# Moving the transposed keys of a gated linear attention forward, waiting for their transfers with one column product, and fixing SyncE's order

## The chip, the cores and the metric

The kernel runs on one core of a Trainium2 chip. Its engines are TensorE (matrix products; the profile shows it as PE, and its weight loads as PEld), VectorE (DVE), ScalarE (ACT), GpSimd (POOL) and SyncE (SP), each with its own queue of instructions that is worked off in order. DMAs are issued from the queues of SP, ACT and POOL. The metric is the time of one execution on the device in microseconds (us).

## The reference

Two blocks follow each other. The first is an attention with a state: for each of 4 batches and 8 heads, with 768 positions and 48 dimensions, a 48x48 state decays by a gate per row and takes up an outer product at every position. The second is a feed-forward net with a leaky activation on the 3072 rows that come out.

```python
def _attn_ref(q, k, v, f_logit):                    # (4, 8, 768, 48) each
    f = 1.0 / (1.0 + np.exp(-f_logit))
    state = np.zeros((B, H, D, D), dtype=np.float32)
    for t in range(S):
        state = f[:, :, t, :, None] * state + np.einsum('bhd,bhe->bhde', k[:, :, t], v[:, :, t])
        y[:, :, t] = np.einsum('bhd,bhde->bhe', q[:, :, t], state)

def _moe_ref(x, w_in, w_out, alpha):                # (3072, 384), (384, 2048), (2048, 384)
    h = x @ w_in
    g = np.maximum(h, 0.0) + alpha * np.minimum(h, 0.0)
    return g @ w_out
```

## The kernel before

**Steps and stages.** The work is cut into 12 steps. A step is a pair of batches (`bp`, 0 or 1) and a chunk of 128 positions (`c`, 0 to 5); the steps run over the chunks, and within a chunk over the two pairs, so that a pair's state is needed again two steps later. Each step has four stages, written as Python generators that yield between pieces:

- `prepare` (letter P; Q is the same for the next step) loads f, q, k and v, takes the sigmoid on ScalarE, and has VectorE make the decayed queries and keys. Its pieces: loads and lagged queries (lines 264 to 296), two scans (317, 319), the products q4 and k4 (321, 347), the decayed keys `ended(0)` into `kh` and `ended(1)` into half of `ks`, among the products `us` (L330) and `q3` (L368); then the other half of `ks` (L398), and, for chunks after the first, a transpose of the 32x32 blocks of `ks` into `kt` (L401); then copies into A on ScalarE (L419) and the transfers of `kt` into `ksn` (L427).
- `carry` (O): products of the half chunks (`off`, L444), then in a second piece the products that update the state (`pd`, L484), 32 small matmuls (each two records in the profile) that read `ksn` and v; VectorE adds them to the state in `vs` (`moved`, L494 and L498).
- `attend` (S): products within blocks (`raw` L520, `qu` L535), their masked copies on VectorE (L526, L541) and ScalarE (L563), the output `py` (L574), its copy `y` (L583), and ten transfers that turn y into rows `xT` for the net (L603), shared out over the queues of SP, ACT and POOL.
- `network` (n) of the step before: eight groups `ph0` to `ph7` of six matmuls with w_in (L618), the activation on ScalarE (L623) and VectorE (L625), then seven products with w_out by a scheme that saves one of eight (`pa` to `pe`, L657), sums (L661, L678), and two stores (L633).

**The transfers of the keys.** `kt` holds the keys with 32x32 blocks transposed; 16 small DMAs on SP put the blocks where the products pd want them. `ksn` has one buffer, and `y` is allocated under the same tag: the transfers of one step wait until the y of the step before has been read by its ten xT transfers, and that y waits for the pd before it.

**Order.** `FIRST` and `USUAL` (lines 31 to 37) spell the order of the pieces: four first steps by themselves, then the usual one. In the step of `USUAL` a step's attention stands between the pieces of the net of the step before and of the preparation of the next. Inside `tc.manual_schedule` (L734) TensorE, VectorE and ScalarE run in just this order; SP and POOL are ordered by a scheduler. The DMAs of loads are issued by POOL, but for the first step's, which SP issues (L262).

**Waits.** A matmul holds one semaphore wait itself; further ones stand in front of it as wait instructions (EVENT_SEMAPHORE) in TensorE's queue, each with up to two. DMAs count on 8 semaphores in turn, so that a DMA also waits for the one eight before it.

**PSUM.** The tag `net` has four banks (ph, pa to pe), the tag `pair` two double banks (raw, qu, off, pd, py).

Of the kernel before, what the change touches and what calls it, by code (L numbers as in the profile page):

```python
# [8 lines left out]
F32 = mybir.dt.float32  # L9
# [18 lines left out]
RAWS, LEADS = 5, 4  # L28
UP = 2.0 ** 16

FIRST = (
# [4 lines left out]
)  # L36
USUAL = "S n2 S n2 O2 n Q n3 Q n Q S3 n Q S n Q n Q n"

def flat(first, usual, steps=12):
    out = []  # L40
    left = {}
    for n in range(steps + 1):
        for key in (first[n] if n < len(first) else usual).split():
            for _ in range(int(key[1:] or 1)):
                k = key[0]
                if k in "awbvW":
                    out.append((k,))
                else:
                    m = n - 1 if k == "n" else n + 1 if k == "Q" else n
                    k = "P" if k == "Q" else k  # L50
                    if 0 <= m < steps:
                        out.append((k, m))
    return out
# [5 lines left out]
def kernel(  # L59
# [65 lines left out]
    def bank(name):  # L125
        return psn.tile([128, 512], F32, tag="net", name=name)
# [131 lines left out]
    def prepare(bp, c, x):  # L258

        i = f"{bp}_{c}"  # L260
        b0 = U * bp
        loads = nc.gpsimd if bp or c else nc.sync  # L262

        def load(name, src, bufs=2):
            t = work.tile([128, W], F32, tag=name, name=f"{name}_{i}", bufs=bufs)
# [105 lines left out]
        def ended(j):  # L371
            js = slice(j, G, 2)
            kj = ks[:, :, 1] if j else kh
            nc.vector.tensor_tensor(kj.rearrange("p g (i r) -> p g i r", r=4),
                                    k4.rearrange("p (g i r) -> p g i r", i=NB, r=4)[:, js],
                                    suf[:, js].unsqueeze(3).broadcast_to((128, GC, NB, 4)), ALU.mult)

        ended(0)
        if c:
            earlier(3)  # L380
        else:
            near(2, 1)
        ended(1)
        if c:
            earlier(4)
        else:
# [8 lines left out]
        yield  # L395
        if c:
            earlier(6)
        nc.vector.tensor_tensor(ks[:, :, 0], kh, f32[:, 1:G:2].broadcast_to((128, GC, DB)), ALU.mult)  # L398
        if c:
            kt = x["kt"] = late["kt"].tile([128, W], F32, tag="kt", name=f"kt_{i}")  # L400
            nc.vector.transpose(kt, ks.rearrange("p g s t -> p (g s t)"))  # L401
            earlier(7)
        else:
            nc.vector.tensor_tensor(q16.rearrange("p g (i r) -> p g i r", r=4), q4[:, :, NQ:NB], g16[:, :, NQ:NB].unsqueeze(3).broadcast_to((128, G, NQ, 4)), ALU.mult)
# [12 lines left out]
        for cc in range(0 if c else 1, NC2):  # L417
            for par in range(2):
                nc.scalar.copy(A[halves(cc)[1], :, par * HP:(par + 1) * HP, CH * cc:CH * (cc + 1)],  # L419
                               q3[rows(par)].rearrange("p (u h c) s t -> p u h c (s t)", h=HP, c=NC2)[:, :, :, cc, 0:CH])  # L420
        if c:
            kt = x["kt"]
            ksn = x["ksn"] = work.tile([128, U, HP * 128], F32, tag="ksn", name=f"ksn_{i}", bufs=1)
            for a in range(4):
                n = min(32, D - 32 * (a % 2))
                for b in range(NJ):
                    nc.sync.dma_start(  # L427
                        out=ksn[32 * b:32 * (b + 1)].rearrange("p u (h x) -> p (u h) x", h=HP)[:, :, 32 * a:32 * a + n],
                        in_=kt[32 * a:32 * (a + 1)].rearrange("p (g b x) -> p g b x", b=NJ, x=32)[:, :, b, 0:n])
        yield  # L430

    def carry(bp, c, x):
# [176 lines left out]
    def network(bp, c, x):  # L609
        i = f"{bp}_{c}"  # L610
        xT = x["T"]
        plain = (bp, c) == steps[0]
        for f in range(NH):
            ph = bank(f"ph{f}_{i}")
            tiles = (2 * f, 2 * f + 1) if plain else (f, f + NH)
            for kt in range(NK):
                for j, m in enumerate(tiles):
                    nc.tensor.matmul(ph[:, j * T:(j + 1) * T], lhsT=w_in_sb[:, kt, m * 128:(m + 1) * 128],  # L618
                                     rhs=xT[:, kt], start=(kt == 0 and j == 0), stop=(kt == NK - 1 and j == 1),
                                     skip_group_check=True)  # L620
            neg = work.tile([128, 2, T], F32, tag="neg", name=f"neg{f}_{i}")
            phv = ph.rearrange("p (j t) -> p j t", j=2)
            nc.scalar.activation(neg, phv, AF.Relu, scale=-1.0)  # L623
            for j, m in enumerate(tiles):
                nc.vector.scalar_tensor_tensor(gate[:, m % NH, m // NH], neg[:, j], om[:, m:m + 1], phv[:, j],  # L625
                                               ALU.mult, ALU.add)
            if not plain and f % 4 == 3:
                sums(slice(f - 3, f + 1))
            yield

        def store(u, o):
            t0 = ((U * bp + u) * NC + c) * C
            nc.sync.dma_start(out=out[t0:t0 + C], in_=o)  # L633

        if plain:
            po = [bank(f"po{u}_{i}") for u in range(U)]
            for n, (f, u) in enumerate([(f, u) for f in range(NF) for u in range(U)]):
                nc.tensor.matmul(po[u][:, 0:DM], lhsT=gate[:, f % NH, f // NH, u * C:(u + 1) * C], rhs=w_out_sb[:, f],  # L638
                                 start=(f == 0), stop=(f == NF - 1))
                if n % 8 == 7 and n != U * NF - 1:  # L640
                    yield
            for u in range(U):
                o = work.tile([128, DM], F32, tag="o", name=f"o{u}_{i}")
                nc.scalar.activation(o, po[u][:, 0:DM], AF.Copy, scale=UP)
                store(u, o)
            yield
            return

        a11, a12, a22 = (lambda f, j=j, u=u: gate[:, f, j, u * C:(u + 1) * C] for j, u in ((0, 0), (1, 0), (1, 1)))
        s1, s2, s3, s4 = (lambda f, n=n: late["S"][:, n, f] for n in range(4))  # L650
        b11, t1, b21, b22 = (lambda f, r=r, d=d: w_out_sb[:, NH * r + f, DH * d:DH * (d + 1)]
                             for r, d in ((0, 0), (0, 1), (1, 0), (1, 1)))
        t2, t3, t4 = (lambda f, t=t: late[t][:, f] for t in ("t2", "t3", "t4"))

        def product(to, of, by, more=False):
            for f in range(NH):
                nc.tensor.matmul(to[:, 0:DH], lhsT=of(f), rhs=by(f), start=(f == 0 and not more), stop=(f == NH - 1),  # L657
                                 skip_group_check=True)

        def plus(to, of, by, scale=UP):  # L660
            nc.vector.scalar_tensor_tensor(to, of[:, 0:DH], scale, by, ALU.mult, ALU.add)  # L661

        o0, o1 = (work.tile([128, DM], F32, tag="o", name=f"o{u}_{i}") for u in range(U))
        kept, u2, u3 = (late["C"][:, n] for n in range(3))
        pa, pb = (bank(f"p{n}_{i}") for n in "ab")
        product(pa, a11, b11)
        product(pb, a22, t4)
        nc.scalar.activation(kept, pa[:, 0:DH], AF.Copy, scale=UP)
        yield
        pc, pd = (bank(f"p{n}_{i}") for n in "cd")  # L670
        product(pc, s2, t2)
        product(pd, s1, t1)
        plus(u2, pc, kept)
        yield
        product(pa, a12, b21, more=True)
        product(pc, s3, t3, more=True)
        plus(o0[:, DH:DM], pd, u2)
        nc.scalar.activation(o0[:, 0:DH], pa[:, 0:DH], AF.Copy, scale=UP)  # L678
        yield
        pe = bank(f"pe_{i}")  # L680
        product(pe, s4, b22)
        plus(u3, pc, kept)
        plus(o1[:, 0:DH], pb, u3, -UP)
        plus(o1[:, DH:DM], pd, u3)
        store(1, o1)
        yield
        plus(o0[:, DH:DM], pe, o0[:, DH:DM])
        store(0, o0)
        yield

    late = {}

    def sums(fs_):

# [36 lines left out]

    pieces["W"] = halves_of_w_out()

    with tc.manual_schedule(engines={mybir.EngineType.PE, mybir.EngineType.DVE, mybir.EngineType.Activation}):  # L734
        for _ in range(IDLE):
            nc.tensor.matmul(idle[0:32, 0:8], lhsT=ones[:, 0:32], rhs=ones[:, 0:8], start=True, stop=True)
        run = {}
        for n, step in enumerate(steps):
            x = {}
            for key, stage_ in zip("POSn", (prepare, carry, attend, network)):  # L740
                run[key, n] = stage_(*step, x)
        for key in order:
            next(run[key] if key in run else pieces[key[0]])
# [55 lines left out]
```

## Time and profile before

| | |
|---|---|
| median of 3 runs | 621.78 us (621.24 to 621.89) |
| span of the profiled execution | 622.1 us |
| instructions in the profile | 19062 |
| ScalarE's share of the chain that ended last | 3% |
| HBM read, written | 36.21 MB, 4.72 MB |

The profile is one execution. It gives busy time per engine, a timeline of instructions, the chain of work that ended last, and for each group of instructions (by line, engine and tile) what ended the idle time before it. A row such as `pd<-vs,ksn` means that the tile pd is written from vs and ksn. A matmul of 32-bit numbers shows as two records. A "q" behind an engine's name (PEldq, SPq) marks work of its sequencer: waits and the issue of DMAs.

Where the loads and transfers stand in the profile before, by its list of DMA issues (KB each, median us from issue to landing):

| transfer | issued by | count | KB | us |
|---|---|---|---|---|
| f | POOL | 11 | 512 | 4.5 |
| q | POOL | 11 | 512 | 4.2 |
| k | POOL | 11 | 512 | 4.9 |
| v | POOL | 22 | 192 | 4.6 |
| ksn from kt | SP | 80 | 32 | 2.0 |
| out | SP | 24 | 192 | 2.7 |

The list groups by shape; the ksn transfers of the other shape, as many again, are not among its eight lines.

### The profile page before, as it was taken

Reading aid. Unit: us, or ns where it says so; the run is one execution under the profiler, and the core shown is the slowest. Engines: PE = TensorE matmul, PEld = TensorE weight load, DVE = VectorE, ACT = ScalarE, POOL = GpSimd, SP = SyncE. Lnnn points to the kernel's source line nnn. Section 1 sums busy time; section 2 is a strip of 40 time slices with the busy share of each in tenths; the row PEclk is TensorE's granted clock in tenths of the full one; section 3 lists DMA queues with packets and bytes.
Section 4 is the critical chain, followed back from the end, with each engine's and each line's share of the span. In section 5 each row is a group of like instructions: output and inputs, shape, how many; then the busy total and the mean of one; then the engine's idle time right before and its main releaser. Section 6 shows DMA issues by size and latency. Waiting matters only on the chain.

```text
span 622.1 us, 19062 instructions
## 1 busy us (share of the span) xinstructions
PE 592.1 (95%) x8212; PEld 529.8 (85%) x8212; DVE 497.1 (80%) x997; ACT 246.6 (40%) x466; POOL 63.0 (10%) x117
## 2 busy tenths in 40 slices
PE   3568999999999999999999999999999999999997
PEld 3457866898899899899899899899889889889997
DVE  7588998899898798798798798798888888762261
ACT  5677862441641272262261351352253243223110
POOL 9120010001000011001001001001001000000000
PEclk9999999999999999999999999999999999999999
DMA  9964632014404314214313313413313401201000
GB/s 290 367 234 155 190 85 52 36 36 108 98 8 96 72 35 107 67 35 95 79 35 90 84 35 88 86 36 86 87 36 85 87 3 26 53 2 27 26 0 26
DMA packets 68116, 50.43 MB, mean 81 GB/s; under 512 B 47168, under 2 KB 60608, under 8 KB 68032
## 3 DMA queue, kind: packets, MB, share of 16 engines
q1 hardware_dynamic: 56656, 25.01, 15.6%
q0 software_dynamic: 6864, 22.35, 12.7%
q10 hardware_dynamic: 4512, 1.85, 1.7%
q8 instruction: 65, 1.06, 0.7%
q14 instruction: 19, 0.16, 0.1%
HBM read 36.21 MB, written 4.72 MB: 66 GB/s over the span
## 4 chain that ended last, share of the span: by engine, by line
PE 88%; DVE 6%; ACT 3%; issue 2%; DMA 1%; ACTq 0%; DVEq 0%
PE ph L618 39%; PE pc L657 9%; PE pa L657 8%; PE pd L657 5%; PE pe L657 4%; PE pb L657 4%; PE py L574 4%; PE po L638 3%; PE raw L520 3%; PE qu L535 3%; PE pd L484 3%; PE off L444 1%; PE xt L592 1%; DVE gate L625 1%; DMA f<-in_fT 1%
## 5 line engine op out<-in xcount | busy, mean ns | idle before, releaser
L618 PE MATMUL ph<-xT,w_in_sb 128*128 128x256 f32 x1152 | 258.7, 382 | 0.7 <-DVE Csum L661 0.7
L618 PEld LDWEIGHTS ph<-xT,w_in_sb 128*128 128x128 f32 x1152 | 216.4, 190 | 33.4 <-issue 2.3
L623 ACT ACTIVATE neg<-ph 128x512 f32<-128x512 f32 x96 | 57.4, 598 | 200.8 <-PE ph L618 139.5
L625 DVE SCALAR_TENSOR_TENSOR gate<-neg,om,ph 128x256 f32<-128x256 f32 x192 | 82.7, 478 | 50.6 <-ACT neg L623 50.4
L657 PE MATMUL pc<-t,S 128*128 128x192 f32 x352 | 61.7, 329 | 0.0
L657 PE MATMUL pa<-w_out_sb,gate 128*128 128x192 f32 x352 | 61.3, 327 | 0.1
L657 PEld LDWEIGHTS pa<-w_out_sb,gate 128*128 128x128 f32 x352 | 57.9, 190 | 1.0 <-DVE gate L625 0.4
L657 PEld LDWEIGHTS pc<-t,S 128*128 128x128 f32 x352 | 57.3, 190 | 0.6
L526 DVE COPY_PREDICATED ad<-mraw,raw 128x256 f32<-128x256 int32 (+1 forms) x96 | 42.4, 442 | 11.1 <-PE raw L520 8.6
L541 DVE COPY_PREDICATED ad<-mquad,qu 128x224 f32<-128x224 int32 (+6 forms) x140 | 42.0, 300 | 6.2
L419 ACT COPY A<-q 48x512 f32<-48x512 f32 x44 | 27.2, 619 | 36.1 <-DVE q L368 35.7
L563 ACT COPY A<-ad 32x256 f32<-32x256 f32 x96 | 38.7, 403 | 1.4
L330 DVE TENSOR_TENSOR us<-us,fs 128x768 f32<-128x768 f32 (+5 forms) x60 | 36.8, 614 | 0.0
L678 ACT ACTIVATE o<-pa 128x192 f32<-128x192 f32 x11 | 3.7, 332 | 75.2 <-PE pa L657 72.3
L661 DVE SCALAR_TENSOR_TENSOR Csum<-pc,Csum 128x192 f32<-128x192 f32 x22 | 7.9, 357 | 30.3 <-PE pc L657 30.1
L287 DVE TENSOR_TENSOR qd<-qd,f 128x768 f32<-128x768 f32 (+2 forms) x36 | 27.2, 756 | 6.0 <-ACT qd L282 6.0
L520 PEld LDWEIGHTS raw<-qd,k 48*32 48x32 f32 x1536 | 18.5, 109 | 15.3 <-issue 13.1
L520 PE MATMUL raw<-qd,k 48*32 48x80 f32 x1536 | 24.0, 243 | 7.6 <-issue 4.4
L702 DVE TENSOR_TENSOR S<-gate 128x512 f32<-128x512 f32 x44 | 30.3, 688 | 0.8
L657 PE MATMUL pe<-w_out_sb,S 128*128 128x192 f32 x176 | 30.4, 326 | 0.0
L657 PE MATMUL pd<-w_out_sb,S 128*128 128x192 f32 x176 | 30.4, 326 | 0.0
L657 PE MATMUL pb<-t,gate 128*128 128x192 f32 x176 | 30.4, 326 | 0.0
(101 smaller groups left out, 758.3 us busy)
## 6 DMA issues: line engine op xcount, KB each, us to landing
w_out_raw<-in_w_out SPq DMA_DIRECT2D x8, 767.8 KB, 5.8
w_in_raw<-in_w_in SPq DMA_DIRECT2D x8, 767.2 KB, 11.9
q<-in_qT POOLq DMA_DIRECT2D x11, 512.0 KB, 4.2
f<-in_fT POOLq DMA_DIRECT2D x11, 512.0 KB, 4.5
k<-in_kT POOLq DMA_DIRECT2D x11, 512.0 KB, 4.9
out<-o SPq DMA_DIRECT2D x24, 192.0 KB, 2.7
vs<-in_v POOLq DMA_DIRECT2D x22, 192.0 KB, 4.6
ksn<-kt SPq DMA_DIRECT2D x80, 32.0 KB, 2.0
```

Source lines behind the costliest of these rows:

```text
L287: nc.vector.tensor_tensor(qdv[d], qdv[d - 1][:, :, :, 1:5 - d], f[:, :, 1:5 - d].rearrange("p (g i) r -> p g i r", i=NB), ALU.mult)
L330: nc.vector.tensor_tensor(us[:, :, UO[m]:UO[m] + 4 * n].rearrange("p g (i r) -> p g i r", r=4), us[:, :, skip:skip + 4 * n].rearrange("p g ...
L419: nc.scalar.copy(A[halves(cc)[1], :, par * HP:(par + 1) * HP, CH * cc:CH * (cc + 1)], q3[rows(par)].rearrange("p (u h c) s t -> p u h c (s ...
L520: nc.tensor.matmul(raw[DB * j:DB * (j + 1), par, hp * C:hp * C + QW], lhsT=k[r_, g * DB:(g + 1) * DB], rhs=qd[r_, g], start=True, stop=True)
L526: nc.vector.copy_predicated(adu[:, :, :, d:4], mraw[:, d, :, d:4].bitcast(I32).unsqueeze(1).broadcast_to((128, H, NB, n)), rv[:, :, QO[d]: ...
L541: nc.vector.copy_predicated(ad[:, u, :, :, 4 * m:DB], mquad[:, lo:lo + n].bitcast(I32).unsqueeze(1).unsqueeze(1).broadcast_to((128, 2, HP, ...
L563: nc.scalar.copy(A[s_, u, :, s_], ad[s_, u].rearrange("p r h t -> p (r h) t"))
L618: nc.tensor.matmul(ph[:, j * T:(j + 1) * T], lhsT=w_in_sb[:, kt, m * 128:(m + 1) * 128], rhs=xT[:, kt], start=(kt == 0 and j == 0), stop=( ...
L623: nc.scalar.activation(neg, phv, AF.Relu, scale=-1.0)
L625: nc.vector.scalar_tensor_tensor(gate[:, m % NH, m // NH], neg[:, j], om[:, m:m + 1], phv[:, j], ALU.mult, ALU.add)
L657: nc.tensor.matmul(to[:, 0:DH], lhsT=of(f), rhs=by(f), start=(f == 0 and not more), stop=(f == NH - 1), skip_group_check=True)
L702: nc.vector.tensor_tensor(to, x_, y_, op)
```

## The change

Four things are changed.

1. From the sixth step on (`ahead >= len(FIRST)`, with a fifth entry START in FIRST) `prepare` computes `ended(1)`, the other half of `ks` and the transpose right behind `ended(0)`, one piece sooner than before.
2. The 16 transfers become a stage of their own, `keys_moved` (M; its step is the next one), placed by hand before the last piece of `prepare`.
3. A new stage `landed` (K), in the usual steps alone (sixth to twelfth), does one matmul of 128 rows: one column of the identity as weights and 4 columns of `ksn` that touch every transfer's bytes. It stands before the group ph3 of the net, in a bank that ph3 then uses; its result is overwritten.
4. From the sixth step on the loads are issued by SP instead of POOL, and SP joins the engines whose order is written out by hand.

```diff
+START = "S n2 S n2 O2 n Q n3 Q n Q S3 n Q S n Q M n Q n"
+
 FIRST = (
         "P5 a2 P a O w S w a w a2 S Q S O S w Q2 S Q2 S w",
-        "a2 w2 n O b w n b2 S P v2 n2 S b v Q n b n O S2 v n b v n Q2 b v Q b n S v2 W Q W S n2 W n",
-        "n S P n2 S W n W n O Q n3 O S Q n S Q n Q S2 Q n3",
-        "S n3 P S Q S n O n O n4 Q S Q S Q n S Q n Q n2",
+        "a2 w2 n O b w n b2 S P v2 n2 S b v Q n b n O S2 v n b v n Q2 b v Q b n S v2 W Q W S M n2 W n",
+        "n S P n2 S W n W n O Q n3 O S Q n S Q n Q S2 Q M n3",
+        "S n3 P S Q S n O n O n4 Q S Q S Q n S Q M n Q n2",
+        START,
 )
-USUAL = "S n2 S n2 O2 n Q n3 Q n Q S3 n Q S n Q n Q n"
+USUAL = "S n2 S n K n O2 n Q n3 Q n Q S3 n Q S n Q M n Q n"
...
-                    m = n - 1 if k == "n" else n + 1 if k == "Q" else n
+                    m = n - 1 if k == "n" else n + 1 if k in "QM" else n
...
-        loads = nc.gpsimd if bp or c else nc.sync
+        ahead = steps.index((bp, c))
+        loads = nc.gpsimd if 0 < ahead < len(FIRST) else nc.sync
...
+        def keys():
+            nc.vector.tensor_tensor(ks[:, :, 0], kh, f32[:, 1:G:2].broadcast_to((128, GC, DB)), ALU.mult)
+            if c:
+                kt = x["kt"] = late["kt"].tile([128, W], F32, tag="kt", name=f"kt_{i}")
+                nc.vector.transpose(kt, ks.rearrange("p g s t -> p (g s t)"))
+
+        sooner = ahead >= len(FIRST)
         ended(0)
+        if sooner:
+            ended(1)
+            keys()
         if c:
             earlier(3)
         else:
             near(2, 1)
-        ended(1)
+        if not sooner:
+            ended(1)
...
-        nc.vector.tensor_tensor(ks[:, :, 0], kh, f32[:, 1:G:2].broadcast_to((128, GC, DB)), ALU.mult)
+        if not sooner:
+            keys()
         if c:
-            kt = x["kt"] = late["kt"].tile([128, W], F32, tag="kt", name=f"kt_{i}")
-            nc.vector.transpose(kt, ks.rearrange("p g s t -> p (g s t)"))
             earlier(7)
...
+    def keys_moved(bp, c, x):
+        kt, i = x["kt"], f"{bp}_{c}"
+        ksn = x["ksn"] = work.tile([128, U, HP * 128], F32, tag="ksn", name=f"ksn_{i}", bufs=1)
+        for a in range(4):
+            n = min(32, D - 32 * (a % 2))
+            for b in range(NJ):
+                nc.sync.dma_start(
+                    out=ksn[32 * b:32 * (b + 1)].rearrange("p u (h x) -> p (u h) x", h=HP)[:, :, 32 * a:32 * a + n],
+                    in_=kt[32 * a:32 * (a + 1)].rearrange("p (g b x) -> p g b x", b=NJ, x=32)[:, :, b, 0:n])
+        yield
+
+    def landed(bp, c, x):
+        to = early[steps[steps.index((bp, c)) - 1]] = bank(f"pw_{bp}_{c}")
+        nc.tensor.matmul(to[0:1, 0:4], lhsT=ident[:, 0:1], rhs=x["ksn"][:, 0, 0:128:32], start=True, stop=True,
+                         skip_group_check=True)
         yield
...
-            ph = bank(f"ph{f}_{i}")
+            ph = early.pop((bp, c), None)
+            if ph is None:
+                ph = bank(f"ph{f}_{i}")
...
-    with tc.manual_schedule(engines={mybir.EngineType.PE, mybir.EngineType.DVE, mybir.EngineType.Activation}):
+    with tc.manual_schedule(engines={mybir.EngineType.PE, mybir.EngineType.DVE, mybir.EngineType.Activation,
+                                     mybir.EngineType.SP}):
```

The same 16 DMAs of `keys_moved` stood in `prepare` before (lines 421 to 429).

More of the change, by code (lines that the diff above doesn't have):

```diff
@@ L420, in prepare @@
                                q3[rows(par)].rearrange("p (u h c) s t -> p u h c (s t)", h=HP, c=NC2)[:, :, :, cc, 0:CH])
[L421 to L429, printed above, removed]
+        yield
[8 more added lines that the diff above has]
+                    in_=kt[32 * a:32 * (a + 1)].rearrange("p (g b x) -> p g b x", b=NJ, x=32)[:, :, b, 0:n])
+        yield
+    def landed(bp, c, x):
+        to = early[steps[steps.index((bp, c)) - 1]] = bank(f"pw_{bp}_{c}")
+        nc.tensor.matmul(to[0:1, 0:4], lhsT=ident[:, 0:1], rhs=x["ksn"][:, 0, 0:128:32], start=True, stop=True,
+                         skip_group_check=True)
         yield
@@ L689, in network @@
         yield
-    late = {}
+    late, early = {}, {}
     def sums(fs_):
@@ L739 @@
             x = {}
-            for key, stage_ in zip("POSn", (prepare, carry, attend, network)):
+            for key, stage_ in zip("POSKMn", (prepare, carry, attend, landed, keys_moved, network)):
                 run[key, n] = stage_(*step, x)
```

## The prediction

> **What bounds the kernel now.** I read the page's busy times and chain of waits first, then the chain in order of time for one step, then the records of the group that looks too long, then the queues that feed it.
>
> ```profile
> PE 592.1 (95%) x8212; PEld 529.8 (85%) x8212; DVE 497.1 (80%) x997; ACT 246.6 (40%) x466; POOL 63.0 (10%) x117
> ...
> PE 88%; DVE 6%; ACT 3%; issue 2%; DMA 1%; ACTq 0%; DVEq 0%
> ```
>
> TensorE is busy 95% of the span and holds 88% of the chain. From the fifth step on it never stands still for another engine: one step follows the next after about 47.7 us. So a gain must make the stream of TensorE shorter; faster transfers or a freer POOL alone give nothing. One step in the chain (start us, length us, what):
>
> ```profile
> 302.50 5.38 PE ph L618 x24
> 307.88 0.71 PE off L444 x50
> 308.59 0.08 issue
> 308.67 1.58 PE pd L484 x63
> 310.25 4.95 PE ph L618 x22
> ```
>
> The group pd L484 (the carried state, 64 small matmul records) takes 1.58 us. The same group in the fourth step, from the timeline, against this one (start, length):
>
> ```profile
> 168.38 0.94 PE L484 MATMUL pd<-vs,ksn 64*48 64x48 f32 x64
> ...
> 308.67 1.58 PE L484 MATMUL pd<-vs,ksn 64*48 64x48 f32 x64
> ```
>
> The work is the same. The view of line L484 has what differs:
>
> ```profile
> L484 PEldq EVENT_SEMAPHORE  x90: 51/51/1734, 33.9 to 547.7; - x90
> ```
>
> These are wait instructions in TensorE's queue, 51 ns each. In the steps from the fifth on nine stand in front of and between the first four matmuls of pd, because those read ksn, which 16 transfers on 8 semaphores fill. In the single records the waits of the fourth step are taken while a ph matmul (216 ns a record) still runs, up to 2.8 us before pd starts, and cost nothing. From the fifth step on pd comes behind off, whose records start 11 ns apart; the queue has no lead left, and each of the four sets of waits opens a hole: pd starts 0.26 to 0.30 us after the last off record, then three more starts come 0.18 us late each.
>
> **The change part by part.**
>
> *The waits leave pd.* I add up, for the seven steps that get a K (sixth to twelfth), the time from the last off record to the first ph record behind pd: 1.792, 1.806, 1.802, 1.781, 1.925, 1.772, 1.807, together 12.69 us. In the built program pd's first matmul keeps a wait for VectorE (copies of qu L541, ended 306.5 here, 2.2 us before pd) and one for TensorE itself, the other 31 none. New length of one: 0.05 into pd (a set of one wait instruction in a fast stream, between raw and qu, gives 0.003 to 0.086), 0.731 from first to last record as in the fourth step, 0.135 from the last pd record to ph as now: 0.916, seven times 6.41. Saved: 6.27 us. Ends: 6.5 if the entry costs 0.011 like any record; 4.7 if the hole at the entry stays (mean 0.278).
>
> *The column product comes in.* One matmul of 4 columns on a one-column weight, two records, between ph2 and ph3. No row shows a small matmul alone between large ones, so I build it from the edges of the small groups: from a ph record to a small one 0.309; from its first to its second record 0.053 (L736, 128x32 weights and 8 columns, back to back); from small to ph 0.122 (off), 0.135 (pd) or 0.186 (qu), I take 0.15; and the second ph record behind a small group starts 0.320 after the first. Together 0.83, where two ph records take 0.432 now: 0.40 a step, 2.80 us in seven. Ends: 0.11 (its two records alone) and 0.58 (its second record held up by 0.18 as pd's are): 0.75 and 4.1 us. Its eight waits are four wait instructions and the matmul's own. They stand behind six large matmuls (12 records, 2.6 us), so 4 x 0.106 us is covered as in the fourth step; without that cover they would cost 0.42 a step. Behind K in TensorE's queue stand ph3, off, pd, all that follows: a late transfer stops everything.
>
> [...]
>
> *Does K find its data?* SyncE's order and VectorE's order around a step (timeline):
>
> ```profile
> 281.50 2.78 SPq L603 DMA_DIRECT2D xT<-y  x4
> 292.01 2.56 SPq L427 DMA_DIRECT2D ksn<-kt  x4
> 295.13 0.34 SPq L633 DMA_DIRECT2D out<-o  x1
> 295.51 8.85 SPq L427 DMA_DIRECT2D ksn<-kt  x12
> 304.48 0.53 SPq L633 DMA_DIRECT2D out<-o  x1
> ```
> ```profile
> 283.53 0.68 DVE L374 TENSOR_TENSOR kh<-k,ss 128x512 f32<-128x512 f32 x1
> ...
> 288.23 1.12 DVE L498 TENSOR_TENSOR vs<-vs,pd 48x384 f32<-48x384 f32 x2
> ...
> 289.97 0.69 DVE L398 TENSOR_TENSOR ks<-kh,ps 128x512 f32<-128x512 f32 x1
> 290.69 1.25 DVE L401 STREAM_TRANSPOSE kt<-ks 128x1024 f32<-128x1024 f32 x1
> 291.85 0.25 DVE L330 TENSOR_TENSOR us<-us,fs 128x128 f32<-128x128 f32 x1
> ```
>
> Today the transposed keys are ready at 291.9, the transfers start at 292.0, and the last lands at 306.7. K stands 2.7 us before off, at 305.1. In the seven steps the last landing stands to that point at +2.3, +1.6, +3.2, +2.8, +1.4, +2.1 and -0.6 us: K without the rest would cost 13.5 us. With the change kh, the other half, ks and the transpose follow each other: 283.5 + 0.6 + 0.6 + 0.7 + 1.25 = 286.7. ksn shares its one buffer with y, so the transfers also wait until y has left as xT. Its landing times now and in the twelfth step, which has no loads beside it:
>
> ```profile
> DMA to landing us min/median/max: 5.2/5.6/5.9
> ...
> DMA to landing us min/median/max: 2.0/2.4/2.9
> ```
>
> The loads of f and v (POOL, 280.0 to 283.5) no longer lie there, so xT should land 4.8 us after its first issue, as in the twelfth step (567.8 to 572.6): 286.3 instead of 288.9. Transfers start near 286.8; 16 issues at 0.655 us on SyncE and 2.0 to land: 298.6, or 6.5 us before K. I cost the wait at nothing; the cover is gone if they start later than 293.3.
>
> *VectorE.* Same instructions, other places: ks and transpose, 1.9 us, now run before the us products L330, L368, the state's L498 and one L661. Up to the last L330 (292.1) the sum is the same, and that is what TensorE's next qu waits for (294.3). The others meet nobody within 1.9 us: raw takes the bank that y's copies free, and the o written at 289.4 is next used at 295.0. Nothing.
>
> *SyncE and POOL.* On SyncE the order is now xT, 16 ksn, two stores, then f, q, k and two v loads. The stores are ready at 295.1 and 295.4 and move to about 297.4; nobody waits for them but the o buffers, a step later. f and q go out near 298.6, k behind raw's second half (301.6), v at about 302.5; at the 5.6 us that f takes now they are there by 304.3, 305, 307.2 and 308.5. ScalarE's sigmoid wants f at 313.7; k is multiplied at about 327. Cover 9 us; each us beyond it would delay VectorE's part of a step, not TensorE at once. xT comes up at 329, long after. POOL keeps two xT moves a step. Nothing.
>
> *The first five steps.* Order on SyncE is fixed there too, but transfers and waits of pd stay; fifth step's pd keeps its 1.77. Nothing.
>
> Sum: 6.27 - 2.80 = 3.5 us of 622.1, the profiled span: 618.6. The runs' median, 621.8, lies 0.3 below that span: **618.3 us**. The far ends, 6.5 - 0.75 and 4.7 - 4.1, give 616.0 and 621.2.
>
> **The rivals.**
>
> *K is nearly free.* Two records, edges hidden by weights loaded ahead: 0.11 a step, saving 5.5, 616.3 us. For it: weight loads overlap (PEld 85% busy under PE). Against: the 0.309 and 0.320 at every edge in the trace. [...]
>
> *The saving is eaten.* The entry's hole stays (4.7) and K costs 0.58 a step (4.1): 0.6 us, 621.2 us. For it: pd's first matmul still carries a wait instruction, and off leaves no lead. Against: the like wait before qu costs under 0.09.
>
> *K waits for ksn: slower.* If the 16 transfers do not start sooner, TensorE stands at K for the 13.5 us added up above and gains 3.5: 631.8 us. It decides from a start later than 6.5 us after the keys are ready. For it: today's margins are negative, one buffer is shared with y, and SyncE now works in a fixed order, so one late item holds the rest. Against: all that stands before ksn on SyncE is ready by 286.8, and no load lies beside.
>
> *The change does not do what it says:* the waits stay at pd. The built program excludes it.
>
> **How the numbers follow.** A measurement tells a change of 0.2% (1.24 us) from none. Forecast (616.8 to 620.3) 0.73; K nearly free 0.11; saving eaten 0.09; K waits 0.07, of which some lies within 0.2% where single steps wait by 1 us. Faster 0.83, same 0.11, slower 0.06. The range, 616.4 to 620.9, takes in the forecast and parts of both neighbours.
>
> **What would show it.** Right: pd in the chain at about 0.87 us from the sixth step on and 1.58 in the fifth; few wait instructions at pd; K's row with a gap of 0.3 to 0.6 us between ph2 and ph3; steps of about 47.2 us; ksn issued near 287 with 16 in a row; POOL's loads four of each. Wrong: an idle time of TensorE before K released by ksn (the slower rival); pd still above 1.1 us (entry); a sigmoid that waits for f on ScalarE; a step that loses elsewhere what pd gained.

## The result and the profile after

The changed kernel takes **618.89 us** (median of 22 runs, 617.33 to 623.58), the kernel before 621.85 us beside it (22 runs, 620.37 to 624.38): a ratio of 0.9959 with a 95% interval of 0.9946 to 0.9973. Two later comparisons of the same program gave 618.61 us (0.9956, interval 0.9941 to 0.9971) and 618.79 us (0.9957, interval 0.9942 to 0.9973). Its profiled execution took 618.04 us, with a span of 616.2. Ratios are taken over fast runs alone, so they need not be the quotient of the medians.

The page's busy times and its chain of waits:

```profile
PE 588.0 (95%) x8226; PEld 525.6 (85%) x8226; DVE 497.4 (81%) x997; ACT 246.0 (40%) x466; POOL 39.1 (6%) x82
...
PE 86%; DVE 6%; ACT 4%; DMA 2%; issue 2%; SPq 0%; ACTq 0%; DVEq 0%
```

TensorE still sets the time. The 14 records more are K's, two in each of seven steps. The chain through the place of the change, in the sixth step (start us, length us, what; pd is now L506, off L466, K L450, the net's large matmuls L642):

```profile
299.62 2.79 PE ph L642 x12
302.40 0.12 PE pw L450 x2
302.53 2.79 PE pw L642 x12
305.31 0.69 PE off L466 x50
306.00 0.86 PE pd L506 x64
306.87 6.24 PE ph L642 x28
```

K stands between two groups of 12 large records, no idle time lies before it, and pd takes 0.86 us. The waits have moved with the need for them. The first line is from the view of L506, the second from that of L450 (duration min/median/max in ns, first and last start in us):

```profile
L506 PEldq EVENT_SEMAPHORE  x35: 51/51/1722, 32.8 to 541.4; - x35
```
```profile
L450 PEldq EVENT_SEMAPHORE  x28: 51/51/51, 252.2 to 535.4; - x28
```

Of the 90 wait instructions at pd 35 are left, and four in each of seven steps belong to K. None of the 28 lasts longer than 51 ns: what they wait for had always landed. Where that comes from shows the timeline of SyncE's queue, then VectorE's:

```profile
278.70 2.60 SPq L625 DMA_DIRECT2D xT<-y  x4
283.98 11.29 SPq L443 DMA_DIRECT2D ksn<-kt  x16
295.37 1.03 SPq L657 DMA_DIRECT2D out<-o  x2
296.44 0.56 SPq L270 DMA_DIRECT2D f<-in_fT  x1
```
```profile
280.74 0.68 DVE L378 TENSOR_TENSOR kh<-k,ss 128x512 f32<-128x512 f32 x1
281.34 0.68 DVE L378 TENSOR_TENSOR ks<-k,ss 128x512 f32<-128x512 f32 x1
281.94 0.68 DVE L383 TENSOR_TENSOR ks<-kh,ps 128x512 f32<-128x512 f32 x1
282.66 1.25 DVE L386 STREAM_TRANSPOSE kt<-ks 128x1024 f32<-128x1024 f32 x1
```

The transpose follows its inputs without a break, the 16 issues go out in one row right behind it, and the last transfer lands at 296.5, 5.8 us before K at 302.3. By the single records this margin is 4.4 to 6.3 us in the seven steps.

### The profile page after: what moved, and what is told of

Read it like the earlier page. It is cut to its first block, busy times and chain, and to the rows that moved or that the text cites. A ratio compares the mean times of both kernels' runs of the same rounds, so it can differ in the third digit from the quotient of the medians.

```text
span 616.2 us, 19049 instructions
## 1 busy us (share of the span) xinstructions
PE 588.0 (95%) x8226; PEld 525.6 (85%) x8226; DVE 497.4 (81%) x997; ACT 246.0 (40%) x466; POOL 39.1 (6%) x82
## 3 DMA queue, kind: packets, MB, share of 16 engines
q10 hardware_dynamic: 4512, 1.85, 1.3%
## 4 chain that ended last, share of the span: by engine, by line
PE 86%; DVE 6%; ACT 4%; DMA 2%; issue 2%; SPq 0%; ACTq 0%; DVEq 0%
PE ph L642 35%; PE pc L681 9%; PE pa L681 9%; PE pd L681 5%; PE pe L681 4%; PE pb L681 4%; PE py L596 4%; PE po L662 3%; PE pw L642 3%; PE raw L542 3%; PE qu L557 3%; PE pd L506 1%; PE off L466 1%; DVE gate L649 1%; PE xt L614 1%
## 5 line engine op out<-in xcount | busy, mean ns | idle before, releaser
L642 PE MATMUL ph<-xT,w_in_sb 128*128 128x256 f32 x1068 | 240.2, 382 | 0.7 <-DVE Csum L685 0.7
L642 PEld LDWEIGHTS ph<-xT,w_in_sb 128*128 128x128 f32 x1068 | 200.0, 190 | 30.9 <-issue 2.2
L647 ACT ACTIVATE neg<-ph 128x512 f32<-128x512 f32 x89 | 53.1, 596 | 179.1 <-PE ph L642 133.8
L649 DVE SCALAR_TENSOR_TENSOR gate<-neg,om,ph 128x256 f32<-128x256 f32 x178 | 76.5, 476 | 37.6 <-ACT neg L647 37.4
L625 POOL DMA_DIRECT2D xT<-y x22 | 11.8, 540 | 393.2 <-ACT y L605 393.2
L542 PEld LDWEIGHTS raw<-qd,k 48*32 48x32 f32 x1536 | 18.5, 109 | 14.1 <-issue 11.9
```

The lines of the kernel that those rows point to most:

```text
L542: nc.tensor.matmul(raw[DB * j:DB * (j + 1), par, hp * C:hp * C + QW], lhsT=k[r_, g * DB:(g + 1) * DB], rhs=qd[r_, g], start=True, stop=True)
```

## The experiments

To compare profiles I leave out the first 200 us and measure one stretch from the records: from the first pd record of the fifth step to the end of the span. The reason is in the part on the hardware.

| kernel | stretch, us | against before, us | ratio of times to before [95%] |
|---|---|---|---|
| before | 408.85 | | |
| changed (three profiles) | 405.28, 405.17, 405.18 | -3.6 | 0.9959, 0.9956, 0.9957 |
| no K | 408.41 | -0.4 | 0.9991 [0.9975, 1.0008] |
| K alone | 424.05, 420.45 | +15.2, +11.6 | 1.0252 [1.0226, 1.0279] |
| K before off | 404.22 | -4.6 | 0.9921 [0.9900, 0.9941] |
| loads on POOL (two) | 404.67, 404.57 | -4.2, -4.3 | 0.9924 [0.9898, 0.9950], 0.9946 [0.9927, 0.9965] |
| keys late | 410.08 | +1.2 | 1.0048 [1.0029, 1.0067] |
| SyncE's order free | 405.00 | -3.9 | 0.9951 [0.9936, 0.9967] |
| K before off, loads on POOL | 403.47 | -5.4 | 0.9922 [0.9906, 0.9939] |

**The changed kernel without K.**

```diff
-USUAL = "S n2 S n K n O2 n Q n3 Q n Q S3 n Q S n Q M n Q n"
+USUAL = "S n2 S n2 O2 n Q n3 Q n Q S3 n Q S n Q M n Q n"
```

> The change without K: keys and transfers as early as in the change, loads on SyncE, SyncE's order fixed. Theory (the gain is the wait instructions that leave pd): pd's waits come back, from the last off record to ph 1.78 us in steps six to twelve as in the kernel before (0.99 in the changed kernel), and no edges of K (0.32 us a step): 3.5 us slower than the changed kernel, that is the time of the kernel before, 621 to 622.5 us. Rival (the gain comes from earlier transfers, from the loads' move or from SyncE's order): it keeps its gain, 618 to 619.5 us.

621.59 us beside 621.59 of before. The chain at pd of the sixth step:

```profile
303.92 0.71 PE off L466 x50
304.62 0.05 issue
304.67 1.58 PE pd L506 x63
306.25 0.41 PE ph L642
```

The transfers are sooner here (the last one of this step lands at 295.1, pd starts at 304.67), and pd is as long as before: it is not the data that is late, it is the wait instructions themselves that cost. So the gain is the place of the waits; sooner keys, SyncE's order and the moved loads, all three without K, gain 0.4 us of the stretch and nothing that the ratio can tell from none.

**The kernel before with K alone.** The stage `landed` and its K are put into the kernel before, at the same place in the steps from the sixth on; keys, transfers, loads and SyncE stay.

```diff
+START = "S n2 S n2 O2 n Q n3 Q n Q S3 n Q S n Q n Q n"
+USUAL = "S n2 S n K n O2 n Q n3 Q n Q S3 n Q S n Q n Q n"
```

> The kernel before with K alone: keys, transfers, loads and SyncE's order as before. Theory: pd shrinks to 0.99 us, but TensorE stands before K until the last transfer has landed, by the margins of the profile before 13.5 us in seven steps, less the 3.5 us gained: 630 to 633 us, with an idle time before K that is released by ksn. Rival (K takes its waits under cover however the transfers lie): 618 to 619.5 us, no idle time before K.

638.09 us. TensorE stands at K in six of seven steps. Against K's usual 0.309 us behind the record before it, the excess is 2.89, 1.68, 2.17, 2.61, 2.39, 2.39 and 0 us, 14.1 together; the margins of before had promised 13.5. But the time is longer than that explains. The chain of the ninth step, then two rows of the view by windows (behind the window, its length and the busy times of PE, PEld, DVE, ACT and POOL: granted clock, DMA share, GB/s):

```profile
404.17 0.04 issue
404.21 2.71 DMA ksn<-kt
406.92 0.47 issue
407.39 0.19 PE pw L435 x2
407.58 4.47 PE pw L627 x12
412.06 0.69 PE off L451 x50
```
```profile
407.40:412.06 4.66, 4.66 (x21) 3.52 (x25) 0.00 (x0) 0.00 (x0) 0.00 (x0) 0.63 0.00 0
358.00:362.70 4.70, 4.70 (x143) 3.96 (x143) 1.29 (x3) 1.86 (x5) 0.00 (x0) 1.00 0.01 3
```

Behind the stall the 12 large records take 4.47 us in place of 2.79, at a mean granted clock of 0.63. This happens in three steps (the stretch from K to pd is 5.28 us there, 3.60 else): 3 x 1.68 = 5.0 us that no theory had. The slower rival of the prediction is thus real for K without the rest, and dearer than its stalls.

**K one group later, right before off, in the bank of ph4.**

```diff
+USUAL = "S n2 S n2 K O2 n Q n3 Q n Q S3 n Q S n Q M n Q n"
```

> The change with K one group of the net later, right before off and in the bank of ph4. Theory (K's price of 0.32 us a step is the edges between large and small matmuls, not its two records of 0.026 us): off has these edges anyway, so K costs some 0.05 to 0.12 us a step and the kernel gains another 1.4 to 1.9 us: 617 to 617.5 us. Rival (the price is K's waits or its own duration, wherever it stands): as the changed kernel, 618.5 to 619.2 us, 0.3 us a step around K.

616.64 us, a little below the 617 to 617.5 expected. The chain:

```profile
303.86 0.65 PE ph L642 x3
304.50 0.12 PE pw L450 x2
304.63 0.69 PE off L466 x50
305.31 0.87 PE pd L506 x64
```

K's own records stand as before (0.309 in, 0.026 between them, 0.098 out), but off starts where it ends and its second record follows 0.007 us behind the first: the way in from a large matmul, which off pays anyway, is shared, and the 0.320 behind is gone. So some 0.12 us a step is left of K's price of 0.321 (worked out below). The stretch is 1.0 us shorter than that of the changed kernel; the edges saved would give 1.4 (7 x 0.2), and the pd of the eighth step is 0.17 us longer than usual in this profile.

**Loads back on POOL.**

```diff
-        loads = nc.gpsimd if 0 < ahead < len(FIRST) else nc.sync
+        loads = nc.gpsimd if ahead else nc.sync
```

> The change with all loads but the first step's on POOL as before. Theory (K has some 6 us to spare, and the loads of f and v beside xT cost 2.5 of them): the transfers start near 289 instead of 287 and land some 4 us before K; no idle time before K, 618.3 to 619.5 us. Rival (the loads have to be out of the way for K): TensorE stands before K by some us in several steps, 620 us or more.

616.40 us, with no stall at K; the time is below the range of the theory too. The move of the loads to SyncE is not needed. Whether it costs something, the second run, beside the changed kernel, was to tell:

> The changed kernel with the loads on POOL once more, beside the changed kernel on one chip. Theory (the loads on SyncE cost 0.3 us at the end and 0.3 us in the steps): 0.6 us less than the changed kernel, the rest of the 2.5 us of the first comparison being the first 75 us of the program. Rival (they cost 2 us or more): 2 us less, and the ratios to before lie apart by 0.3%.

> The changed kernel beside the one with the loads on POOL: 618.6 us, ratio to before 0.9956.

617.07 us (0.9946) against 618.79 (0.9957); the intervals overlap. In the profiles the stretch is 0.6 us shorter than the changed kernel's, 0.31 of it behind the last matmul: from there to the end of the span are 3.28 to 3.29 us in every kernel here with the loads on POOL, before among them, and 3.59 to 3.60 in every one with the loads on SyncE. The rest lies in the group qu: over the stretch, from its first record to the next group's, it takes 14.12 and 14.14 us with the loads on POOL and 14.65, 14.45 and 14.34 in the changed kernel's three profiles. But it takes 14.11 in the kernel with SyncE's order free (below), where SyncE issues the loads too, so this part is not shown to be a cost of the loads. The difference of the ratios, 0.0011 or 0.7 us, is of the size of the 0.6, that of the medians (1.7 us) is not. A cost of 0.3 us at the end is what the profiles show; more is open.

**The keys in their old place, the rest of the change kept.**

```diff
-        sooner = ahead >= len(FIRST)
+        sooner = False
```

> The changed kernel with the keys' other half, ks and the transpose back in their old place in VectorE's order; the loads stay on SyncE behind the transfers. The transposed keys are then ready near 291.9 instead of 286.7 on the clock of the sixth step before. Theory (the sooner keys only buy spare time, most of which is not used): 16 issues of 0.655 us and 2.0 us to land end at 304.4, against K at 305.1: 0.7 us to spare, so stalls of 0 to 0.5 us a step and a time of 619 to 622 us. Rival (the sooner keys are what lets K pass): K stands by 1 us or more in each of seven steps, above 626 us.

624.85 us: slower than before, and between the two theories. The stalls at K in the profiled execution (621.65 us, the shortest of six) are 0.71, 0.18, 0, 1.61, 0.65, 0.45 and 0 us, 3.6 together. The largest, in the chain:

```profile
395.16 1.85 SPq L443
397.01 0.04 issue
397.05 1.86 DMA ksn<-kt
398.91 0.24 issue
399.15 0.19 PE pw L450 x2
```

The last of the 16 issues takes 1.85 us where 0.61 is usual (another of this step took 1.62). My 0.7 us to spare counted 16 issues at the median; single ones that are late use it up. So the sooner keys are not a reserve that nobody uses: without them the change loses. In this profile the stalls of 3.6 us take back the whole gain of the stretch, and a hole of 1.15 us in one pd (last section) makes it longer than that of before; the 3.2 us by which the median lies above the profiled run are in no profile.

**SyncE out of the hand-written order.**

```diff
-    with tc.manual_schedule(engines={mybir.EngineType.PE, mybir.EngineType.DVE, mybir.EngineType.Activation,
-                                     mybir.EngineType.SP}):
+    with tc.manual_schedule(engines={mybir.EngineType.PE, mybir.EngineType.DVE, mybir.EngineType.Activation}):
```

> The changed kernel without SyncE's fixed order; the built program then issues the 16 transfers still in a row, and the stores and loads in another order around them. Theory (SyncE's order has 6 us to spare at K and 9 at the loads): the same time as the changed kernel within 0.2%, 618 to 620 us, and no idle time before K. Rival (the fixed order is needed): K waits for ksn, or ScalarE's sigmoid for f, 621 us or more.

617.67 us, no stall at K, the stretch 0.2 to 0.3 us shorter than the changed kernel's: fixing SyncE's order is not needed either.

**The changed kernel again, and K before off with the loads on POOL.** The second joins the edits of two experiments above.

> The changed kernel itself, beside the next one on the same chip. 618.9 us; the first 75 us of its profile are expected to differ by 1 to 3 us from those of the earlier profile of the same program, while the step to step period stays at 47.10 to 47.17 us.

> The changed kernel with K one group later, right before off and in the same bank as ph4, and with the loads back on POOL. Theory (a price at each edge between large and small matmuls; where the loads are issued is worth nothing): the time of the run with K before off and the loads on SyncE, 616.6 us, thus 2.2 us below the changed kernel. Rival (the loads on SyncE cost something in each step, as the run with the loads on POOL suggested by 616.4 against 618.9): both gains add up, 614.2 us.

618.61 and 615.90 us. The second is the shortest stretch of all, 1.1 us below that with the loads on POOL alone. Its ratio of 0.9922 equals that of K before off with loads on SyncE: 615.9 lies nearer to the theory's 616.6 than to the rival's 614.2. The stretch, however, is 0.75 us below that of K before off, 0.31 of it behind the last matmul again: the two gains do add up, but the one from the loads is small. Of the first expectation a part fell: the changed kernel's three profiles differ by only 0.6 us in their first 75 us, and its periods from the sixth step on are 47.03 to 47.16 us, where 47.10 to 47.17 were expected.

**K alone, once more.**

> The kernel before with K alone once more. In its first profile TensorE stood 2.0 to 3.2 us at K in six steps, and behind three of these stalls (2.92, 2.70 and 2.69 us, the ninth to eleventh step) 12 matmuls ran at a granted clock of 0.63 and took 1.7 to 1.9 us longer, behind the other three (3.20, 1.98 and 2.48 us) none did. Theory (the clock is granted from activity in windows of fixed length, and a stall of 2 to 3 us loses it only where it fills most of one): stalls of the same lengths, but the slow matmuls behind another set of them; each time 1.7 us. Rival (something in the ninth to eleventh step does it): the same three steps again.

One execution, 631.74 us. Stalls of 1.87, 1.90, 1.55, 2.20, 2.56, 2.28 and 0 us over the usual, 12.4 together; the slow matmuls stand in the tenth and eleventh step alone, 1.61 and 1.56 us dearer. By windows, behind the tenth step's stall and behind the ninth's:

```profile
452.40:457.00 4.60, 4.60 (x40) 3.35 (x42) 0.00 (x0) 0.20 (x1) 0.00 (x0) 0.63 0.00 0
402.60:406.50 3.90, 3.90 (x106) 3.23 (x110) 0.24 (x1) 0.82 (x2) 0.00 (x0) 1.00 0.00 0
```

The set is another one, so the rival falls, though two of its three steps come again; the theory's windows of fixed length stand in the clock's own record (last section). Counted from the record before K, the stalls with a lower clock behind them are 2.59 to 2.92 us in both profiles, those without 1.86 to 2.51 and, once, 3.20.

## Why the prediction held

**The waits leave pd: right, 0.54 us too large.** The stretch from the last off record to the ph record behind pd is now 0.987, 0.988, 0.988, 0.987, 1.032, 0.988 and 0.988 us: saved 5.73 us, where 6.27 stood in the sum (its ends 4.7 and 6.5). The stream (0.730) and the way out (0.135) came as taken; the mis-sized part is the entry, 0.122 in place of 0.05. I had taken it from a wait instruction in a fast stream. It is the edge between two groups instead, the same 0.122 that the prediction itself read between off and ph. The kernel without K shows that the saving belongs to the wait instructions.

**The column product: right in kind, 0.55 us too dear.** 0.309 in and 0.320 to the second large record behind came as read from other edges. Between its records there are 0.026 us (taken: 0.053) and from it to the large matmul 0.098 (taken: 0.15). That is 0.321 a step, 2.25 us in seven, against 0.40 and 2.80. The edges are what K before off saves. Small records alone are not dear: pd's start 0.0116 us apart on average (0.730 us from the first to the last of 64), and the price of K is twelve times the distance of its two.

**The sum.** 5.73 - 2.25 = 3.48 us; the prediction had 3.47. That it is so near is luck: both terms were half a microsecond too large, with opposite signs. The stretch of the first profile closes with two more terms that the sum did not have: qu, py and raw together are 0.39 us shorter, and the time behind the last matmul is 0.30 us longer, which makes 3.57.

**K finds its data: right, and its rival was the one to fear.** The first issue comes at 283.98, right behind the transpose, and the margin is 4.4 to 6.3 us, where 6.5 was predicted. The rival "K waits for ksn" has its point of decision where I put it: with the old transfers (K alone) it costs 12.4 to 14.1 us of stalls. The term that it lacked is the granted clock behind a stall, 3.2 to 5.0 us more. In the forecast I named three things that bring the data sooner (the transpose, the loads out of the way, SyncE's order). The runs separate them: without the sooner transpose K stalls, while each of the other two can be left out by itself (both at once was not tried).

**The moves at no cost: nearly.** VectorE's new order delays nothing that the steps show. In the step shown f lands at 300.6, and ScalarE's sigmoid takes it at 310.4, right behind its own work. Only the loads on SyncE cost 0.3 us, behind the last matmul, where I had looked at nothing; a further 0.3 us in the steps is not shown to be theirs.

**From the profile to the median.** I wrote that the median lay 0.3 us below the span. In every kernel here a run's time is its span plus 1.8 us (616.2 and 618.04), so the profiled execution of before took about 623.9 us, 2.1 above its median. Its second pd starts at 73.5, that of the changed kernel at 71.3. A difference of spans (5.9 us) would therefore have told a wrong gain; the sum by steps did not depend on it. The profiles' stretch gives 3.6 us, the medians 3.0, the ratios 2.6 with an interval of 1.7 to 3.4. What is missing to 3.6 is not shown by any run; the start of the program, which varies by more, is the first suspect.

## What to carry to other kernels

Waits cost time here where the engine's queue had no lead, not only where the data was late: pd's cost 0.82 us a step (5.73 us in seven). A cheap instruction that takes the waits behind long matmuls (K, 0.32 us a step) can be worth more than faster data (without K all of it gained 0.4 us of the stretch), if the data is there several microseconds ahead in every step (4.4 to 6.3 us here), late issues included. What K cost was its edges to the large matmuls (0.32 us a step between two large groups, some 0.12 right before off), so such a tiny matmul belongs next to a group that already has such an edge. When several moves come together, run each alone: here the waits' new place and the sooner transpose made the gain, and each of the two other moves could be left out by itself.

## What the runs showed of the hardware

- **A short stall can cost the clock.** In the two profiles of K alone TensorE's granted clock was 0.63 to 0.64 over the next 4.6 us behind five stalls of 2.59 to 2.92 us, and each cost 1.56 to 1.68 us on top; behind a stall of 3.20 us it stayed at 1.00. The clock's record in these profiles shows more. Each loss is one stretch of 3.41 us at a granted clock of 0.50, half of which is 1.7 us, and from where the record of 1.00 begins (at 49.55 and 47.43 us) to the first loss behind a stall there are 358.40 and 406.19 us, that is 105 and 119 times 3.413. In the profiles of before and of the changed kernel, which lose nothing in their spans, the record holds 1.00 from 49.76 us on for 573.44 us and from 47.48 us on for 570.03 us, 168 and 167 times 3.413. In these four profiles the clock thus changes on a fixed grid of 3.413 us, which the stalls do not move. The first profile of K alone, by windows of this grid: the two around the first loss, then the two that share the stall of 3.20 us.

```profile
404.53:407.95 3.42, 0.88 (x6) 0.52 (x5) 2.11 (x8) 0.60 (x1) 0.00 (x0) 1.00 0.45 113
407.95:411.36 3.41, 3.41 (x10) 2.70 (x9) 0.00 (x0) 0.00 (x0) 0.00 (x0) 0.50 0.00 0
...
254.35:257.76 3.41, 2.35 (x11) 1.71 (x10) 3.03 (x10) 0.60 (x1) 0.00 (x0) 1.00 0.76 203
257.76:261.17 3.41, 1.65 (x9) 1.49 (x10) 0.96 (x3) 0.00 (x0) 0.00 (x0) 1.00 0.07 24
```

In the five windows just before a loss PE's records were busy 0.88 to 1.45 us of the 3.41; of the windows from the sixth step on that kept the clock, in both profiles, one had 1.42 and all others 1.61 or more. So the length of a stall alone does not decide. What goes with a loss in these rows is how little TensorE does within one window, which was idle throughout in none of the five; where the limit lies they tell only roughly.

- **The first 75 us vary.** The two profiles of K alone have their second pd at 72.89 and 69.83; from there to the fifth pd both need 139.6 us.
- **A hole inside pd that no wait explains.** With the keys late, one pd of the eighth step stopped for 0.87 us, in the chain "issue":

```profile
353.00 0.76 PE pd L506 x52
353.76 0.87 issue
354.63 0.38 PE pd L506 x12
```

This pd is 1.15 us longer than usual by its records. No wait instruction stands there, and the 16 DMA engines were busy all through that microsecond with the loads (a share of 1.03). That alone does not explain it: in five other steps of this run their share was 1.02 to 1.13 during pd, and pd took its usual 0.73 us. The cause stays open.
